# A fused attention and feed-forward kernel on one core: a new written-out order, with GpSimd squares in the first batch alone and seven products for the first row pair

## The chip, the cores and the metric

The kernel runs on one core of a Trainium2 chip. The core has TensorE (matmuls, PE in the profile), VectorE (DVE), ScalarE (ACT), GpSimd (POOL), and SyncE (SP), which here only issues transfers. Each engine takes its instructions strictly in the order of its own queue; a semaphore holds an instruction until what it needs is there. The metric is device time in microseconds of one execution; the median of three is given.

## The reference

Inputs q, k and v are 8 batches x 12 heads x 448 positions x 64. For each head, `scores = q k^T / 8`, `attn = max(scores, 0)^2 / 448`, `out = attn v`. The heads of a position are laid side by side to a row of 768, which gives 3584 rows. A feed-forward part follows: `h = x w_in` (768 to 2048), `g = h * sigmoid(1.702 h)`, `y = g w_out` (2048 to 768). Output is 3584 x 768 in float32. Products are in float16 with float32 sums.

## The kernel before

**Units.** Attention goes by units of four heads: 8 batches x 3 units, unit u = 3 * batch + part. A unit's 448 positions are seven blocks j of 64. For a unit, k and q are brought to float16 and transposed; then for each j four 64x64-tiled matmuls fill two PSUM banks with scores (`scores`, L143, word `s`), two ReLUs bring them to float16 in SBUF (`relu`, L156, word `r`, on ScalarE or VectorE), and one square in place makes the weights (`square`, L165, word `x`, on ScalarE, VectorE or GpSimd). When all seven are squared, `attn_v` (L173, word `a`) runs 28 matmuls, and `xt_evac` (word `e`) copies the result into the transposed activations of the feed-forward part.

**Ways in for k and q.** Units 0 to 5 load by a casting transfer on GpSimd's queue (`jk`, `jq`; unit 0 by SP and a cast) and transpose on TensorE (`tk`, `tq`) with a copy out (`ek`, `eq`). From unit 6 on SP loads float32 (`Lk`, `Lq`, one staging buffer each), an engine casts (`K`, `Q`; L107), and SP issues a DMA transpose (`Rk`, `Rq`). v is always a casting transfer on GpSimd's queue (`V`). Weights come by GpSimd's queue too (`jwa`, `jwb`, `jo`). The word `G` makes SP wait for a part of the weights, so that its later loads don't start earlier.

**Groups.** The feed-forward part takes positions in eight groups of 384 and 512 rows by turns (`gblk`, 6 and 8 blocks). The hidden layer of group 0, and half of group 1's, is a plain product (`m1`, word `f`); the rest uses seven products where eight would be needed: `unit_product` (word `u`, products 0 to 6) with sums of weights (`s_sum`, `S`) and of activations (`t_sum`, `T`) made beforehand, snapshots of a bank between products (`t`) and additions (`b`). Then gelu on ScalarE (`g`) and `widen`, a scaling into float16, on GpSimd (`v`).

**Output.** Rows go in tiles of 128. A pair of tiles takes seven products of eight matmuls (`pair_product`, L375, word `p`) with row sums on VectorE (`a_sum`, L357, word `A`), sums of the output weights (`w_sum`, `W`), copies out (`h`) and final adds (`l`). A tile without a partner is either plain (`m2`, word `m`, with `n` for the copy out: 16 matmuls for each half of the columns) or `single` (word `i`, also 16, with one sum `A.5` of its own). `o` and `q` issue the stores.

**Order.** There is no scheduler at run time: a string of some 1,900 words is the program. `do` (L441) executes them in turn, and each engine's queue is the subsequence of words that fall to it. A word is a name with numbers, then an engine after a colon where it isn't the default (a, d, p for ScalarE, VectorE, GpSimd), then PSUM banks after @. Defaults are in `home`: ScalarE for ReLUs, snapshots, copies out and k casts, GpSimd for widening and q casts, VectorE for the rest. There are eight banks; a word with @ waits until the bank's last reader is done. Tiles of a pool rotate over its buffers in the order in which the words ask for them.

Of the kernel before, what the change touches and what calls it, by code (L numbers as in the profile page):

```python
# [15 lines left out]
def kernel(  # L16
# [406 lines left out]
    with tc.manual_schedule():  # L423
# [35 lines left out]
        def zeros(e, p, n):  # L459
# [8 lines left out]
            "Lk0 z13@0 jk1 V1 jq1 I V0 K0:d tk0@1 z1 ek0 jk2 Lq0 Q0:a tq0@2 eq0 tk1@3 s0.3@4.5 "  # L468
            "r0.3.1 jq2 ek1 s0.1@6.7 r0.1.0 r0.3.0:d s0.0@0.1 s0.2@2.3 tq1@5 r0.0.1:d r0.2.0 "
            "s0.5@4.6 r0.1.1 s0.4@1.2 r0.0.0 r0.5.1 s0.6@7.0 eq1 r0.4.0:d tk2@5 x0.0 s1.0@1.6 "  # L470
            "r0.4.1 x0.4 jwb2 r0.5.0 x0.5 r0.6.1 jk3 r0.2.1 r0.6.0 x0.3:p jq3 x0.1 ek2 r1.0.1 "
            "r1.0.0 x0.2 x0.6 s1.5@2.4 s1.2@0.3 r1.2.0 s1.1@7.6 r1.1.1 tq2@5 a0@1.0 r1.1.0 r1.5.0 "
            "s1.6@6.7 eq2 r1.2.1 x1.0 r1.5.1 r1.6.0 s1.3@5.2 r1.3.0 x1.1 x1.2 tk3@3 e0.0.0 "
            "e0.0.1:a jk4 x1.5 e0.1.0:a tq3@4 r1.3.1 ek3 eq3 jwb0 x1.3 jq4 jwa0 s1.4@6.5 r1.6.1 "
            "V2 x1.6 r1.4.1 r1.4.0 s2.0@1.3 s2.2@2.7 r2.2.1 e0.1.1:a s2.1@4.5 r2.0.1 r2.0.0 "
            "r2.2.0 tk4@6 r2.1.1 x1.4 a1@7.0 e1.0.1:a ek4 r2.1.0:d x2.2 s2.6@3.6 r2.6.0 tq4@1 "
            "r2.6.1 e1.0.0 s2.3@2.4 r2.3.0 e1.1.1 x2.0 x2.1 eq4 s2.4@5.0 r2.3.1 jwa1 s2.5@3.6 "
            "f0.2.0@2 r2.4.0 r2.4.1 jwb1 jwa2 jq5 f0.3.0@4 s3.0@1.5 x2.6 e1.1.0 x2.3 f0.3.1 x2.4 "
            "jk5 r2.5.0 r2.5.1 x2.5 r3.0.0:d S0.1 V3 f0.2.1 f0.0.0@7 f0.0.1 s3.1@0.3 r3.0.1 "
            "a2@6.5 jwb3 r3.1.1:d r3.1.0 s3.2@1.0 e2.0.0 f0.1.0@3 e2.0.1:a r3.2.1 r3.2.0 G3 "  # L480
            "e2.1.1:a e2.1.0 x3.0 f0.1.1 f0.1.2 g0.1 x3.1:p V4 f0.2.2 s3.5@6.0 r3.5.0:d g0.2 "
            "s3.4@1.5 f0.0.2 v0.1 f0.3.2 r3.4.0 V5 r3.4.1 f0.4.0@3 r3.5.1:d x3.2 x3.5 g0.3 g0.0 "
            "f0.4.1 s3.3@2.6 s3.6@1.0 jwa3 f0.8.0@5 r3.3.1 r3.6.0 v0.0 r3.3.0 f0.4.2 g0.4 f0.8.1 "
            "f0.8.2 s4.1@4.7 s4.3@6.1 r3.6.1:d s4.0@0.2 f0.6.0@3 f0.6.1 r4.1.0 r4.3.1 x3.6 V9 "
            "f0.6.2 r4.3.0 x3.3 f0.5.0@4 r4.1.1:d r4.0.1:d x3.4 f0.5.1 S0.2 x4.1 f0.5.2 v0.4 "
            "s4.2@7.1 x4.3 a3@2.6 g0.8 g0.5 r4.2.1:d s4.4@5.4 r4.2.0 r4.0.0 tq5@7 g0.6 v0.2 jo1.0 "
            "Lk6 r4.4.0:d r4.4.1 tk5@0 eq5 s4.5@1.3 s4.6@4.5 ek5 e3.0.1:a f0.11.0@6 x4.2:a "
            "f0.7.0@7 f0.11.1 f0.11.2 r4.6.1:d r4.5.0 r4.5.1:d r4.6.0:d f0.10.0@0 f0.10.1 f0.7.1 "
            "x4.6 e3.0.0:a jo0.0 x4.5:a x4.4 f0.10.2 S2.1 g0.11 s5.1@1.5 s5.0@2.3 x4.0:p v0.5 "
            "f0.7.2 v0.11 f0.14.0@4 r5.0.1:d v0.6 f0.14.1 g0.10 r5.1.0 r5.1.1 r5.0.0 f0.14.2 "  # L490
            "jo0.1 S1.1 g0.14 g0.7 s5.4@6.0 a4@1.3 s5.3@5.2 r5.4.0:d v0.7 r5.3.0 e4.0.0:a "
            "s5.2@4.7 r5.4.1:d r5.2.1:d f0.12.0@6 x5.0:p e4.0.1:a f0.13.0@0 r5.2.0:d f0.12.1 "
            "f0.12.2 x5.4:a g0.12 v0.3 f0.15.0@5 f0.15.1 s5.5@7.1 r5.5.1 s5.6@4.3 r5.3.1:d x5.3 "
            "r5.5.0:d r5.6.0:d f0.13.1 r5.6.1 jo1.1 f1.7.0@2 f0.13.2 f1.1.0@6 x5.1:p v0.12 v0.10 "
            "v0.14 K6:p x5.5:a g0.13 f0.15.2 f1.5.0@1 f1.5.1 f1.7.1 S2.2 S2.4 x5.2:a x5.6:a "
            "f0.9.0@7 f0.9.1 f0.9.2 f1.4.0@3 S2.3 g0.15 g0.9 a5@4.0 e5.0.1:a f1.0.0@5 f1.0.1 "
            "f1.3.0@7 f1.1.1 Lq6 Q6:a e5.0.0 T1.1 T1.2 S1.2 v0.13 f1.7.2 g1.7 f1.3.1 v1.7 v0.9 "
            "Lq7 f1.3.2 f1.4.1 f1.4.2 f1.5.2 Rk6 u1.2.0@0 f1.6.0@4 Rq6 S3.1 g1.5 f1.6.1 g1.3 "
            "f1.2.0@2 f1.0.2 f1.6.2 v1.3 v0.15 t1.2.0 S3.3 g1.0 v0.8 g1.6 v1.0 Lk7 T1.4 S3.2 g1.4 "
            "u1.2.2 S3.4 W2.1 f1.2.1 f1.2.2 S1.4 u1.3.0@1 v1.4 W1.1 Q7:a f1.1.2 g1.1 v1.5 v1.1 "  # L500
            "u1.2.1@7 b1.2.1 g1.2.1 v1.2.1 v1.6 m0.0.0@5 u1.2.3 g1.2 s6.2@4.3 T1.3 Lq8 t1.3.0 "
            "s6.1@6.2 u1.3.2 S0.3 t1.2.2 n0.0.0:a r6.2.0 u1.2.4 r6.1.1:d r6.2.1:d s6.0@5.4 r6.0.1 "
            "r6.0.0 x6.0:a t1.3.2 V11 t1.2.4:d W0.1 u1.3.1@2 W2.2 Rq7 W0.2 m0.0.1@3 K7:p Q8:a "
            "b1.3.1 b1.2.3 g1.2.3 Rk7 u1.2.5 u1.2.6 u1.3.4 r6.1.0 W3.1 S0.4 v1.2 V7 u1.3.3 g1.2.5 "
            "v1.2.3 s6.4@4.5 s6.3@6.0 S1.3 n0.0.1 t1.3.4 g1.3.1 b1.2.6 b1.3.3 s6.5@3.7 r6.4.0 "
            "u1.3.5 x6.1:p r6.3.0:d r6.4.1:d r6.5.0 W1.2 v1.3.1 v1.2.5 u1.3.6 Lk8 g1.3.5 W3.2 V6 "
            "x6.4:a r6.3.1:d x6.2:a r6.5.1 Rq8 b1.3.6 K8:p m0.1.0@4 s6.6@6.3 W2.4 v1.3.5 g1.3.3 "
            "v1.3.3 s7.2@5.1 g1.2.6 x6.3 W1.4 v1.2.6 Lq9 g1.3.6 s7.0@0.2 r7.2.1 r7.0.0 x6.5:a Q9 "
            "r6.6.1:d r7.2.0:d Lk9 r7.0.1 m0.1.1@7 r6.6.0:d n0.1.0:a Rk8 s7.1@3.1 x6.6 W3.4 "
            "x7.0:a a6@5.0 s7.3@6.2 r7.1.0:d r7.1.1 n0.1.1 Lq10 s7.4@4.3 x7.2 e6.0.1:a K9:p "  # L510
            "r7.3.1 e6.1.1:a e6.0.0 r7.4.0:d p1.0.0@1 o0.0 r7.4.1:d e6.1.0:a s7.6@7.2 s7.5@0.5 "
            "r7.3.0 x7.1 x7.3 r7.6.0 r7.6.1:d r7.5.0 s8.2@4.6 m0.2.0@3 r7.5.1 r8.2.0:d V10 x7.4 "
            "s8.1@7.0 x7.6 r8.2.1 x7.5:a h1.0.0 n0.2.0:a s8.0@5.6 r8.1.1 a7@2.4 v1.3.6 r8.0.1 "
            "A1.0.1@0 A1.0.2@1 s8.3@3.0 W0.4 r8.3.0 r8.1.0:d e7.0.1 e7.1.1:a r8.3.1 p1.0.1@6 "
            "s8.5@7.3 V8 e7.0.0:a r8.0.0:d x8.1 e7.1.0 r8.5.0:d Rk9 r8.5.1 Rq9 s8.6@4.5 x8.0 x8.2 "
            "r8.6.1 x8.3:a p1.0.2 x8.5 r8.6.0:d s8.4@0.2 r8.4.1 s9.0@3.7 r8.4.0 l1.0.1 r9.0.0 "
            "x8.6 r9.0.1 x8.4 x9.0:a m0.2.1@5 n0.2.1:a s9.1@2.4 A1.0.4 r9.1.1:d Lk10 r9.1.0 "
            "a8@0.3 s9.2@7.5 e8.0.0:a Q10:d e8.0.1:a s9.3@4.2 r9.2.1:d r9.3.1 K10:p p1.0.3 "
            "u2.0.0@5 r9.2.0 Rk10 u2.1.0@2 Lk11 K11:p T2.1 W3.3 e8.1.0 T2.2 T2.3 e8.1.1:a "
            "s9.4@7.3 u2.0.1@0 W1.3 r9.4.1:d t2.0.0 u2.0.2 b2.0.1 t2.1.0 u2.1.2 u2.1.1@3 r9.3.0:d "  # L520
            "b2.1.1 W0.3 T2.4 r9.4.0 t2.0.2 u2.0.3 u2.0.4 g2.0.1 v2.0.1 t2.1.2 u2.2.0@7 g2.1.1 "
            "t2.0.4 b2.0.3 Lq11 t2.2.0 v2.1.1 u2.1.4 t2.1.4 h1.0.2 x9.2 u2.1.3 b2.1.3 u2.2.1@4 "
            "u2.0.6 g2.0.3 v2.0.3 b2.2.1 x9.4:a u2.2.2 u2.1.6 b2.0.6 g2.2.1 g2.0.6 Rq10 W2.3 "
            "u2.2.3 u2.3.0@0 Q11:a b2.1.6 t2.2.2:d u2.0.5 v2.0.6 g2.1.6 u2.3.1@3 g2.1.3 t2.3.0:d "
            "b2.3.1 v2.1.6 v2.2.1 u2.2.4 u2.1.5 u2.3.2 u2.3.3 t2.2.4 u2.2.5 A1.0.3 b2.2.3 u2.2.6 "
            "Lk12 o0.1 g2.3.1 t2.3.2 v2.3.1 v2.1.3 g2.0.5 g2.1.5 v2.0.5 u2.3.4 p1.0.4 g2.2.3 "
            "g2.2.5 s9.6@5.2 v2.1.5 b2.2.6 s9.5@4.7 t2.3.4:d u2.3.5 x9.1:a v2.2.3 K12 Lq12 b2.3.3 "
# [147 lines left out]
```

## Time and profile before

| | |
|---|---|
| median of 3 runs | 369.43 us (369.36 to 370.56) |
| the profiled execution's own time | 369.32 us |
| its span, first to last instruction | 367.5 us |
| granted TensorE clock | 0.998 |
| TensorE busy, 3570 matmuls | 357.2 us |
| VectorE busy | 290.2 us |
| ScalarE busy | 276.8 us |
| GpSimd busy | 179.0 us |
| HBM read and written | 45.6 and 11.0 MB |

A busy time is the union of the engine's instructions, so instructions that overlap count once. In a row of the timeline or of the groups, `at<-sc` means that tile `at` is written from tile `sc`: `sc` scores, `at` weights, `av` attention output, `xe`/`xo` activations of even and odd groups, `ht`/`hx` hidden layer in PSUM, `gf` the same in SBUF, `ge`/`go` after widening, `ox`/`op`/`os` outputs of pairs, plain tiles and singles, `osb` outputs in SBUF, `asum` row sums, `winS`/`wT` weight sums. All matmuls of the feed-forward part have the helper's line L203, all two-input sums L88.

### The profile page before, as it was taken

To read this page: it belongs to the slowest core of one execution; us is meant where nothing else is said; L and a number is where in the kernel's file an instruction comes from. 1 tells how busy PE (TensorE), PEld (TensorE's weight loads), DVE (VectorE), ACT (ScalarE), POOL (GpSimd) and SP (SyncE) were. 2 spreads that over 40 slices of the span, in tenths; PEclk is the share of its full clock that TensorE was granted. 3 is DMA by queue.
4 is the path that set the end of the run, shared out by engine and by line. 5 is a ranking of instruction groups with operands and counts; after the bars stand their busy time and mean duration, and the time that the engine had idled before them with its cause. 6 is when DMAs were issued, how large, how long until landed. Compare 5 with 4: busy or idle time off the path is not lost.

```text
span 367.5 us, 9086 instructions
## 1 busy us (share of the span) xinstructions
PE 357.2 (97%) x3570; PEld 231.1 (63%) x3570; DVE 290.2 (79%) x519; ACT 276.8 (75%) x542; POOL 179.0 (49%) x229
## 2 busy tenths in 40 slices
PE   7899999999999999999999999999999999999994
PEld 4454545664569555886559755786549755787662
DVE  3999968599997877878898788767887899755642
ACT  3998976687888998889958898878995897174310
POOL 6838695674115585256404856367342536043300
PEclk9999999999999999999999999999999999999999
DMA  9999999799964885978583396368943042300244
GB/s 197 195 205 204 241 209 219 129 172 207 130 179 118 165 236 98 204 164 186 102 167 73 98 199 136 102 146 162 239 98 77 0 112 28 87 0 2 70 114 119
DMA packets 65228, 51.39 MB, mean 140 GB/s; under 512 B 35745, under 2 KB 61857, under 8 KB 65185
## 3 DMA queue, kind: packets, MB, share of 16 engines
q1 hardware_dynamic: 48256, 36.32, 42.4%
q0 software_dynamic: 16608, 14.09, 25.5%
q8 instruction: 28, 0.46, 0.5%
q10 hardware_dynamic: 320, 0.39, 0.4%
q14 instruction: 16, 0.12, 0.1%
HBM read 45.61 MB, written 11.01 MB: 154 GB/s over the span
## 4 chain that ended last, share of the span: by engine, by line
PE 84%; DVE 10%; ACT 2%; DMA 1%; issue 1%; POOL 1%; SPq 0%; POOLq 0%; DVEq 0%; ACTq 0%
PE hx L203 29%; PE ox L203 26%; PE sc L150 9%; PE ht L228 7%; PE av L181 7%; PE os L203 4%; DVE at L88 3%; PE op L203 3%; DVE at L161 2%; ACT at L163 2%; DVE wT L88 1%; DMA qst<-in_q_dram 1%; DVE asum L88 1%; POOL ge L217 1%; POOL at L88 1%
## 5 line engine op out<-in xcount | busy, mean ns | idle before, releaser
L163 ACT ACTIVATE at<-sc 128x448 f16<-128x448 f32 x215 | 104.7, 567 | 13.2 <-PE sc L150 12.8
L161 DVE TENSOR_SCALAR at<-sc 128x448 f16<-128x448 f32 x121 | 71.8, 618 | 12.9 <-PE sc L150 12.5
L217 POOL TENSOR_SCALAR go<-gf 128x512 f16<-128x512 f32 x64 | 41.6, 650 | 64.0 <-ACT gf L214 47.2
L88 DVE TENSOR_TENSOR gf<-hx,gf 128x512 f32<-128x512 f32 (+1 forms) x78 | 47.9, 627 | 26.8 <-PE hx L203 14.2
L203 PEld LDWEIGHTS <-win 128*128 128x128 f16 x624 | 56.4, 98 | 8.4 <-issue 2.8
L88 POOL TENSOR_TENSOR at<-at 128x896 f16<-128x896 f16 x27 | 45.7, 1694 | 29.8 <-ACT at L163 18.0
L217 POOL TENSOR_SCALAR ge<-gf 128x384 f16<-128x384 f32 x64 | 35.8, 559 | 45.9 <-ACT gf L214 28.7
L169 ACT ACTIVATE at<-at 128x896 f16<-128x896 f16 x57 | 53.9, 955 | 0.9 <-DVE at L161 0.6
L150 PE MATMUL sc<-qT,kT 64*64 64x448 f16 x672 | 52.4, 359 | 2.2 <-DVE at L161 0.6
L88 DVE TENSOR_TENSOR at<-at 128x896 f16<-128x896 f16 x84 | 53.7, 673 | 0.8 <-ACT at L163 0.4
L214 ACT ACTIVATE gf<-gf 128x512 f32<-128x512 f32 (+1 forms) x78 | 43.2, 579 | 9.4 <-DVE gf L88 9.4
L203 PE MATMUL ox<-wout,go 128*128 128x384 f16 x256 | 46.5, 327 | 0.0
L203 PEld LDWEIGHTS <-winS 128*128 128x128 f16 x468 | 42.7, 98 | 4.5 <-issue 1.0
L203 PEld LDWEIGHTS <-go 128*128 128x128 f16 x320 | 29.9, 98 | 22.6 <-issue 4.8
L203 PEld LDWEIGHTS <-ge 128*128 128x128 f16 x288 | 27.5, 98 | 19.7 <-issue 3.3
L79 ACT ACTIVATE gf<-hx 128x512 f32<-128x512 f32 (+1 forms) x51 | 27.2, 543 | 15.3 <-PE hx L203 7.2
L203 PE MATMUL hx<-T,winS 128*128 128x256 f16 (+1 forms) x312 | 37.0, 261 | 0.0
L181 PE MATMUL av<-at,v 64*64 64x448 f16 x672 | 36.2, 350 | 0.6 <-DVE at L88 0.4
L150 PEld LDWEIGHTS <-kT 64*64 64x64 f16 x672 | 17.7, 105 | 27.9 <-issue 23.5
L203 PE MATMUL hx<-xo,win 128*128 128x256 f16 x252 | 32.1, 273 | 0.0
L203 PE MATMUL ox<-wT,asum 128*128 128x384 f16 x176 | 31.8, 327 | 0.0
L203 PEld LDWEIGHTS <-asum 128*128 128x128 f16 x200 | 18.7, 98 | 15.3 <-issue 3.1
(78 smaller groups left out, 481.6 us busy)
## 6 DMA issues: line engine op xcount, KB each, us to landing
out_dram<-osb SPq DMA_DIRECT2D x52, 192.0 KB, 3.3
kst<-in_k_dram SPq DMA_DIRECT2D x19, 448.0 KB, 5.2
qst<-in_q_dram SPq DMA_DIRECT2D x19, 448.0 KB, 4.2
v<-in_v_dram POOLq DMA_DIRECT2D x24, 224.0 KB, 5.4
win<-in_moe_w_in_dram POOLq DMA_DIRECT2D x8, 384.0 KB, 9.5
wout<-in_moe_w_out_dram POOLq DMA_DIRECT2D x4, 768.0 KB, 12.3
k<-in_k_dram POOLq DMA_DIRECT2D x5, 224.0 KB, 6.5
q<-in_q_dram POOLq DMA_DIRECT2D x5, 224.0 KB, 6.0
```

The source lines that it names most:

```text
L79: nc.scalar.activation(out=o, in_=i, func=AF.Copy)
L88: eng[e].tensor_tensor(out=o, in0=x, in1=y, op=op)
L150: nc.tensor.matmul(out=sc[a][c, 0:S], lhsT=st["kT"][r, j, c], rhs=st["qT"][r, :, c], start=True, stop=True)
L161: nc.vector.tensor_scalar(out=o, in0=i, scalar1=0.0, scalar2=None, op0=ALU.max)
L163: nc.scalar.activation(out=o, in_=i, func=AF.Relu)
L169: nc.scalar.activation(out=at, in_=at, func=AF.Square)
L181: nc.tensor.matmul(out=av[s][64 * a:64 * a + 64, 0:S], lhsT=v16[r, a, 64 * j:64 * j + 64], rhs=at[r, a, :], start=(j == 0), stop=(j == J - 1))
L203: nc.tensor.matmul(out=o, lhsT=lhs(i), rhs=rhs(i), start=start and i == 0, stop=i == n - 1, skip_group_check=True)
L214: nc.scalar.activation(out=o, in_=i, func=AF.Gelu_apprx_sigmoid, scale=1.0 / SC)
L217: eng[e].tensor_scalar(out=o, in0=i, scalar1=SC, scalar2=1.0, op0=ALU.mult, op1=ALU.mult)
L228: nc.tensor.matmul(out=hp[g, f][:, 0:n], lhsT=w[:, i, fo:fo + 128], rhs=xts[g][:, i, 0:n], start=i == 0, stop=i == NK - 1)
```

## The change

Only the string of words changes (1,939 words before, 1,950 after). Functions stay as they are. Three things differ in the words.

Squares on GpSimd (`x...:p`) stay in the first batch alone, units 0 to 2: four, where 27 lay over the whole program. Casts of k and q (`K`, `Q`) may go to any of three engines. Group 0's three output tiles, plain before (`m0.*`, `n0.*`), become one pair in seven products and one single:

```diff
-            "x6.4:a r6.3.1:d x6.2:a r6.5.1 Rq8 b1.3.6 K8:p m0.1.0@4 s6.6@6.3 W2.4 v1.3.5 g1.3.3 "
...
+            "l0.0.1 u1.3.3 u1.2.6 s6.3@1.7 W0.4 x6.1:a p0.0.2 W1.3 b1.2.6 Rq8 g1.2.3 r6.3.0:d "
+            "t1.3.2 s6.5@4.1 A0.0.4 h0.0.2:d r6.3.1 u1.3.4 W0.3 v1.2.3 p0.0.3 Q7:a v1.6 r6.5.0 "
...
+            "v1.3.1 b1.3.3 x6.3 V7 s6.4@1.6 r6.4.0 p0.0.4 u1.3.6 h0.0.4:d u1.3.5 Rq7 r6.6.1 "
+            "l0.0.3 r6.4.1:d b1.3.6 p0.0.5 g1.2.6 g1.3.5 s7.4@7.1 s7.0@4.6 g1.3.6 g1.3.3 v1.3.3 "
```

And all words stand in a new order, with new banks and, in part, other engines. The first words:

```diff
-            "Lk0 z13@0 jk1 V1 jq1 I V0 K0:d tk0@1 z1 ek0 jk2 Lq0 Q0:a tq0@2 eq0 tk1@3 s0.3@4.5 "
-            "r0.3.1 jq2 ek1 s0.1@6.7 r0.1.0 r0.3.0:d s0.0@0.1 s0.2@2.3 tq1@5 r0.0.1:d r0.2.0 "
...
+            "jq1 z13@0 Lk0 I K0:d tk0@1 ek0 z1 Lq0 Q0:a tq0@2 tq1@3 jk1 eq0 s0.1@4.5 jwb2 jk2 "
+            "s0.6@6.7 s0.4@0.1 r0.4.0:d r0.6.0 tk1@2 ek1 jq2 jq3 eq1 s0.3@6.0 r0.1.1 r0.4.1 "
```

Counted over the whole program:

| words | before: ScalarE / VectorE / GpSimd | after |
|---|---|---|
| squares `x` | 57 / 84 / 27 | 72 / 92 / 4 |
| ReLUs `r` | 215 / 121 / 0 | 201 / 135 / 0 |
| casts `K`, `Q` | 14 / 2 / 22 | 16 / 4 / 18 |
| snapshots `t` | 51 / 27 / 0 | 44 / 34 / 0 |
| row sums `A` | 0 / 47 / 0 | 0 / 52 / 0 |
| copies out `h`, `n`, `l.5` | 35 / 21 / 0 | 37 / 19 / 0 |
| adds at the end `l` | 0 / 33 / 0 | 0 / 36 / 0 |
| matmuls of group 0's output | 96 of 384 columns | 88 of 384 columns |

In the first batch, up to the word `a2` ScalarE had 39 ReLUs and no square, VectorE 5 ReLUs and 20 squares, GpSimd 1 square; after, ScalarE has 31 ReLUs and 5 squares, VectorE 15 and 12, GpSimd 4 squares.

## The prediction

> **What bounds the kernel now.** I read the page first: the busy shares and the 40 slices.
>
> ```profile
> PE 357.2 (97%) x3570; PEld 231.1 (63%) x3570; DVE 290.2 (79%) x519; ACT 276.8 (75%) x542; POOL 179.0 (49%) x229
> ...
> PE   7899999999999999999999999999999999999994
> ...
> DVE  3999968599997877878898788767887899755642
> ACT  3998976687888998889958898878995897174310
> ```
>
> TensorE is busy 97%, but [...] this share hides stalls. The chain of waits gives issue rates instead: 8 matmuls of 384 columns take 1.30 us (0.163 each), 4 score matmuls 0.19, the 28 of one attention product 1.32, a 192-column matmul 0.083, a 256-column one 0.109. Times the counts in the groups, all matmuls need about 336 us (168 score groups 31.9, 24 attention products 31.7, transposes and warm-up 8.5, 504 + 588 gated products 106, first group's hidden layer 26, 808 output matmuls 131). The span is 367.5; the tail after the last matmul is 4.8 us and the head 1.2. So some 25 us are stalls. Stretches cut at the attention products of units 2, 3, 5, 6 and 8 (PE, PEld, DVE, ACT, POOL busy) show where:
>
> ```profile
> 0.00:26.70 26.70, 22.69 (x318) 12.39 (x322) 21.03 (x41) 20.57 (x46) 17.41 (x28) 1.00 1.13 199
> 26.70:36.70 10.00, 9.81 (x104) 4.79 (x100) 9.89 (x18) 8.24 (x20) 7.55 (x11) 1.00 1.26 204
> 53.60:86.30 32.70, 32.31 (x253) 19.50 (x253) 25.16 (x41) 23.99 (x43) 20.91 (x27) 1.00 0.97 174
> 86.30:103.20 16.90, 16.21 (x164) 8.45 (x167) 16.83 (x32) 12.96 (x29) 4.25 (x5) 1.00 1.05 162
> ```
>
> First place: from the first cast at 4.3 us to 36.7 us VectorE has no idle time to speak of, while the matmuls there need some 25 us. VectorE sets the start. Second place: 77 to 103 us, VectorE full again (16.83 of 16.90). From 103 to 313 us TensorE sets the pace with 1 to 2 us of stall per stretch; the last 50 us are TensorE alone.
>
> The groups give the prices of what the change moves between engines (busy, then mean ns of one):
>
> ```profile
> L163 ACT ACTIVATE at<-sc 128x448 f16<-128x448 f32 x215 | 104.7, 567 | 13.2 <-PE sc L150 12.8
> L161 DVE TENSOR_SCALAR at<-sc 128x448 f16<-128x448 f32 x121 | 71.8, 618 | 12.9 <-PE sc L150 12.5
> L88 POOL TENSOR_TENSOR at<-at 128x896 f16<-128x896 f16 x27 | 45.7, 1694 | 29.8 <-ACT at L163 18.0
> L169 ACT ACTIVATE at<-at 128x896 f16<-128x896 f16 x57 | 53.9, 955 | 0.9 <-DVE at L161 0.6
> L88 DVE TENSOR_TENSOR at<-at 128x896 f16<-128x896 f16 x84 | 53.7, 673 | 0.8 <-ACT at L163 0.4
> ```
>
> These overlap by about 0.1 us when they follow each other. In the timeline 19 ReLUs of ScalarE take 8.40 us, so one costs (8.40 - 0.57)/18 = 0.435; two ScalarE squares take 1.81, so 0.855 for the second; three VectorE squares 1.69, so 0.535; two VectorE ReLUs 1.16, so 0.54. Moving a square from VectorE to ScalarE frees 0.535 and costs 0.855; the ReLU that goes back frees 0.435 and costs 0.54.
>
> VectorE squares average 673 ns, 55 above their usual 618. The timeline shows why:
>
> ```profile
> 10.62 2.86 DVE L88 TENSOR_TENSOR at<-at 128x896 f16<-128x896 f16 x4
> ...
> 29.00 1.80 DVE L88 TENSOR_TENSOR at<-at 128x896 f16<-128x896 f16 x1
> ...
> 78.83 2.60 DVE L88 TENSOR_TENSOR wT<-wout,wT 128x768 f16<-128x768 f16 x2
> ```
>
> Four squares should take 3 x 0.535 + 0.618 = 2.22, and take 2.86 while a GpSimd square runs (9.68 to 11.39). One alone takes 1.80 beside a GpSimd square from 28.65. Two weight sums, which should take 1.02, take 2.60 beside GpSimd widenings. Summed over all VectorE operations that read two SBUF tiles, the lengthening is 11.8 us: 3.2 beside GpSimd squares, 4.7 beside widenings, 1.5 beside casts, the rest not clearly placed.
>
> [...]
>
> **The change, part by part.**
>
> Group 0's first pair. Before, three plain tiles: 3 x 2 x 16 = 96 matmuls of 384 columns. After: 7 x 8 = 56 for the pair, 2 x 16 = 32 for the tile left over, 88. Saved 8 x 0.163 = 1.3 us, where TensorE sets the pace. Added on VectorE: five sums of 0.60 (3.0 us, between 55 and 90 us), and three fused adds for copies (near nothing). The pair also needs the sums of the output weights (16 x 0.47 = 7.5 us) some 20 us earlier. Those weights are four loads of 12.3 us from issue to landing; the last is now asked for behind more widenings, so the first sums may wait 1 to 2 us on VectorE. Nothing waits behind them then: in the 10 us that follow VectorE has 4 us less work than TensorE. I count 0 (to +1).
>
> The first batch. Counted in order of issue up to unit 2's attention product: VectorE has 1 cast, 10 transposed copies, 5 ReLUs and 20 squares (36 x 0.535), a weight sum and four small copies: 20.9 us. After: 1, 10, 15 and 12 (38 x 0.535) and three copies: 21.4. ScalarE goes from 39 ReLUs to 31 ReLUs and 5 squares: 18.8 to 19.7. GpSimd squares there go from 1 to 4. Each of the two seen by 30 us lengthened VectorE, by 0.64 and 1.18; three more at 0.6 each, since not every one meets a square, add 1.8. So VectorE reaches that point 0.5 + 1.8 = 2.3 us later. Bounds: nothing, if the three meet ReLUs [...]; 4, if each costs 1.2. By unit 5's product TensorE has been the bound in the old kernel with 3 us of VectorE slack, so a part is given back: I take **+1.5** (0 to +3). Loads don't decide: the new GpSimd queue asks for q and k of units 1 to 3 before v, and at the old 1.1 us per load v of unit 0 lands near 15 us, ahead of its use.
>
> 53 to 103 us. GpSimd loses the square at 76.15 that stood among blocked weight sums. Against that, five sums, and every square after batch 0 on the other two. Counting issue costs between the products of units 5 and 8: VectorE 37.3 before, 39.6 after, TensorE's bare columns 44.1 and 43.7. Before, VectorE's work came late and was lengthened by 4.8 us, most of it between 77 and 90 us; after, it is spread evenly. I take **-0.5** (-2.5 to +2).
>
> Steady stretches. GpSimd drops 23 squares (37 us); 15 go to ScalarE, 8 to VectorE, and 14 ReLUs and 7 snapshots pass from ScalarE to VectorE. VectorE's issue total rises 264 to 284 us, ScalarE's 256 to 262: both below TensorE's 326 bare columns, so the cover holds on average. It is thinnest between the products of units 12 and 14: VectorE 17.0 us, ScalarE 15.6, bare TensorE 15.3, in 16.9 us before (there VectorE 13.5). Early work in the stretch before must hide it. **+0.7** (-0.5 to +2.5).
>
> Banks. A bank is free about 0.2 us after its last matmul's columns plus the copy (0.49 to 0.69) plus 0.05: 0.75 to 0.96. Counting TensorE work between the last write of a bank and its next use beyond 60 us, the old order has nothing under 0.96. The new has nine places at 0.56 to 0.85 (after unit-product 2.2.4, single product 4.2.1, pair products 5.0.5 and 5.0.6 and others). Deficits of 0.1 to 0.3 each: **+0.8** (+0.2 to +2).
>
> SP's queue. Casts k and q change engines, and unit 7's q comes late: its cast stands after the product 0.0.3 on ScalarE, then SP must issue unit 9's q load (0.4) and the DMA transpose (4.1 us to landing): 0.95 + 0.4 + 4.1 = 5.5 us. TensorE has 4.2 us of columns before unit 7's first scores; everything behind them on TensorE waits. The cast can run up to 1.3 us early. **+0.3** (0 to +1.5). Other units have over 6 us.
>
> Tail: same last products, one evacuation and stores. 0.
>
> Sum: -1.3 + 1.5 - 0.5 + 0.7 + 0.8 + 0.3 = +1.5 us. The profiled run took 369.3 us (span 367.5 and 1.8 around it), 0.1 under the median of 369.43, so the change stands for both: 369.4 + 1.5 = **370.9 us**.
>
> **Rivals.** (1) Faster, by one mechanism: VectorE's blocked time. If the early GpSimd squares cost VectorE nothing (unit 2's product starts by 27 us) and the spread of weight sums takes out the 77 to 103 us plug (-2.5), and the last three entries come to 1.0 instead of 1.8, the sum is -1.3 + 0 - 2.5 + 1.0 = -2.8: 366.6. It decides from 0.8 us saved in the plug on: -1.3 - 0.8 + 1.0 = -1.1. For it: 4.8 of the 11.8 us of lengthening lie around that plug. Against: five more sums on the same engine. (2) VectorE and ScalarE become the bound in the attention stretches: with 17.0 of VectorE work where 16.9 us passed, six stretches lose 0.7 more each: 375. Against: the average slack. (3) Nothing measurable: the start's loss is given back before unit 5, as TensorE then has work stored up: -1.3 + 0.3 - 0.5 + 0.7 + 0.8 + 0.3 = +0.3, 369.7.
>
> **Numbers.** My forecast (slower by 0.3 to 1%) 0.43, rival 2 0.14, rival 3 0.25, rival 1 0.18. A measurement of this kernel can tell 0.3% (1.1 us) from no change. Faster 0.18, same 0.25, slower 0.57. The range reaches to half of rival 1 and all but the worst of rival 2: 367.8 to 374.5; the forecast's own range is 370.5 to 373.
>
> **What will show it.** In the new profile: 88 matmuls into the group-0 output, unit 2's attention product near 29 us (26.7 before) with VectorE squares over 1 us beside GpSimd squares; GpSimd near 140 us busy; VectorE busy over 295; a TensorE wait before unit 7's first scores near 83 us; short waits after the nine bank places. Wrong, if unit 2's product comes by 27 us, or if the last stretch (313 us on) moved by itself.

## The result, and the profile after

The changed kernel takes 370.71 us (median of 20 runs, 367.98 to 374.67); the old one, run beside it, 369.77 us (20 runs, 368.98 to 372.12). The ratio of comparable runs is 0.9999, 95% interval 0.9978 to 1.0021: no difference that can be measured. Four of the changed kernel's runs, 374.0 to 374.7 us, were in a slow state and don't count in the ratio; the first profile was taken in one of them (374.0 us, granted clock 0.987), so unless said otherwise "the changed kernel" is read from a second execution of the same words (370.7 us, span 368.9, clock 0.993; 22 more runs, median 370.61, ratio 1.0004, interval 0.9982 to 1.0025).

Its page, lines of parts 1, 2 and 5:

```profile
PE 357.8 (97%) x3562; PEld 232.7 (63%) x3562; DVE 302.2 (82%) x556; ACT 281.2 (76%) x540; POOL 136.9 (37%) x202
...
PE   8699999999999999999999999999999999999994
...
DVE  3978996999987889787997989798897899856452
ACT  3979985789988999889897898778887899245210
...
PEclk9989999999999999999999999999999999999999
...
L88 DVE TENSOR_TENSOR at<-at 128x896 f16<-128x896 f16 x92 | 56.7, 638 | 1.7 <-ACT at L163 0.6
```

Work moved as counted: 8 matmuls fewer, GpSimd from 179 to 137 us, VectorE from 290 to 302. VectorE's squares average 638 ns where they took 673. But in the third slice, 18 to 28 us, VectorE and ScalarE fall from 9 and 9 to 7 and 7: they wait where they were full. And there the granted clock is below 0.9 (0.50 from 19.0 to 22.4 us).

The same execution cut at the attention products of units 2, 3, 5, 6 and 8 (the columns are again PE, PEld, DVE, ACT, POOL busy, then clock, DMA share and GB/s):

```profile
0.00:30.76 30.76, 24.92 (x318) 13.01 (x318) 21.96 (x43) 22.14 (x44) 20.78 (x29) 0.94 1.13 193
...
57.78:88.98 31.20, 31.12 (x247) 18.42 (x250) 28.27 (x50) 23.88 (x45) 14.71 (x22) 1.00 0.89 179
88.98:104.20 15.22, 15.22 (x165) 7.94 (x160) 13.79 (x28) 14.74 (x29) 5.59 (x8) 1.00 0.95 217
```

Unit 2's product stands at 30.76 us instead of 26.70, with as many matmuls before it (318). The stretch from unit 5 to unit 8 takes 46.42 us (31.20 + 15.22) where it took 49.66 (53.57 to 103.23), and VectorE is no longer full in its second part (13.79 of 15.22). So "no change" is a loss and a gain of the same size. Starts of TensorE's groups, from the traces:

| start of, us | before | changed | difference | changed, first profile |
|---|---|---|---|---|
| unit 2's product | 26.68 | 30.76 | +4.1 | 30.30 |
| unit 5's product | 53.57 | 57.78 | +4.2 | 57.33 |
| unit 8's product | 103.23 | 104.20 | +1.0 | 107.56 |
| last matmul | 362.54 | 363.94 | +1.4 | 367.11 |

The first profile loses almost 4 us more between units 5 and 8, most of it at one place, to which the last experiment comes back.

What TensorE waited for between 8 and 35 us, in the list of waits (us in total, times, longest):

```profile
PE tr L131 <- DMA q<-in_q_dram: 1.3, 1, 1.3
PE av L181 <- DMA v<-in_v_dram: 0.9, 1, 0.9
PE tr L131 <- DMA k<-in_k_dram: 0.9, 1, 0.9
```

Three loads lead the list; the two entries below them are 0.6 and 0.2 us. In the same window of the old kernel only one load stood there, with 0.3 us:

```profile
PE sc L150 <- DVE kT L83: 0.4, 1, 0.4
PE tr L131 <- DMA q<-in_q_dram: 0.3, 1, 0.3
```

By the trace TensorE was ready for q of unit 2 at 12.9 us, for k of unit 3 at 15.7 and for v of unit 0 at 17.5; they landed at 14.2, 16.6 and 18.4. In the old order q of unit 2 landed at 12.5, k of unit 3 at 16.2 but was wanted only after unit 0's product, and v of unit 0 was there at 9.8. An input-weight block, asked for third on GpSimd's queue, now stands ahead of them.

And the contention that the prediction put on the first batch is not there. GpSimd's squares, then VectorE, in the timelines of the changed kernel:

```profile
17.97 1.71 POOL L88 TENSOR_TENSOR at<-at 128x896 f16<-128x896 f16 x1
...
25.12 5.41 POOL L88 TENSOR_TENSOR at<-at 128x896 f16<-128x896 f16 x3 [3.07 <-ACT at L163]
```

```profile
23.50 2.22 DVE L88 TENSOR_TENSOR at<-at 128x896 f16<-128x896 f16 x4
...
26.17 2.77 DVE L161 TENSOR_SCALAR at<-sc 128x448 f16<-128x448 f32 x5
```

Four squares take 2.22 us, the undisturbed time that the prediction worked out. From 25.12 to 30.53, while GpSimd squares, VectorE finishes the last of the four and then has ReLUs and copies from PSUM, which keep their usual lengths: five ReLUs in 2.77 us (4 x 0.54 + 0.62 = 2.78), two more in 1.16, copies of 0.61 and 0.62. Beside the single square from 17.97 it has one copy of 0.61 us.

### The profile page after: what moved, and what is told of

It is laid out like the page before. It is cut to its first block, busy times and chain, and to the rows that moved or that the text cites. A ratio compares the mean times of both kernels' runs of the same rounds, so it can differ in the third digit from the quotient of the medians.

```text
span 372.2 us, 9025 instructions
## 1 busy us (share of the span) xinstructions
PE 358.6 (96%) x3562; PEld 233.2 (63%) x3562; DVE 302.9 (81%) x556; ACT 281.3 (76%) x540; POOL 137.6 (37%) x202
## 4 chain that ended last, share of the span: by engine, by line
PE 84%; DMA 7%; DVE 3%; POOL 2%; ACT 1%; issue 1%; SPq 0%; DVEq 0%; ACTq 0%
PE ox L203 30%; PE hx L203 27%; PE sc L150 9%; PE av L181 8%; PE os L203 6%; DMA wout<-in_moe_w_out_dram 4%; PE ht L228 3%; DMA v<-in_v_dram 2%; DMA qst<-in_q_dram 1%; DVE wT L88 1%; PE tr L131 1%; POOL ge L217 1%; DVE at L88 1%; ACT gf L214 1%; POOL go L217 0%
## 5 line engine op out<-in xcount | busy, mean ns | idle before, releaser
L163 ACT ACTIVATE at<-sc 128x448 f16<-128x448 f32 x201 | 99.6, 559 | 13.0 <-PE sc L150 12.7
L161 DVE TENSOR_SCALAR at<-sc 128x448 f16<-128x448 f32 x135 | 79.8, 618 | 10.9 <-PE sc L150 10.6
L169 ACT ACTIVATE at<-at 128x896 f16<-128x896 f16 x72 | 68.2, 962 | 1.7 <-DVE at L161 1.2
L88 DVE TENSOR_TENSOR at<-at 128x896 f16<-128x896 f16 x92 | 55.9, 631 | 1.7 <-ACT at L163 0.6
L181 PE MATMUL av<-at,v 64*64 64x448 f16 x672 | 37.5, 357 | 1.0 <-DMA v<-in_v_dram 1.0
L203 PEld LDWEIGHTS <-ge 128*128 128x128 f16 x256 | 24.0, 98 | 18.4 <-issue 4.1
L79 ACT ACTIVATE gf<-hx 128x384 f32<-128x384 f32 (+1 forms) x44 | 23.3, 537 | 15.4 <-PE hx L203 12.0
L203 PE MATMUL ox<-wT,asum 128*128 128x384 f16 x192 | 34.9, 327 | 0.0
L203 PEld LDWEIGHTS <-asum 128*128 128x128 f16 x224 | 21.1, 98 | 16.3 <-issue 3.3
L81 ACT ACTIVATE osb<-ox 128x384 f32<-128x384 f32 x32 | 15.4, 496 | 19.2 <-PE ox L203 19.1
```

The source lines that it names most:

```text
L79: nc.scalar.activation(out=o, in_=i, func=AF.Copy)
L81: nc.scalar.activation(out=o, in_=i, func=AF.Copy, scale=scale)
L88: eng[e].tensor_tensor(out=o, in0=x, in1=y, op=op)
L161: nc.vector.tensor_scalar(out=o, in0=i, scalar1=0.0, scalar2=None, op0=ALU.max)
L163: nc.scalar.activation(out=o, in_=i, func=AF.Relu)
L169: nc.scalar.activation(out=at, in_=at, func=AF.Square)
```

## The experiments

Theory: the order of the first 30 us, with its loads, costs some 3 to 4 us, and the rest of the changed kernel is better than the old one by as much. Rivals: the elementwise engines set the start (the prediction's step); the losses were accidents of one execution; the squares' engines decide. All diffs are of words; a word that moves is shown at both places. Ratios are to the old kernel, with 95% intervals.

### The changed kernel again

No edit.

> The changed kernel once more, nothing edited, for a profile at full granted clock (the first one had 0.987) and a second interval. Theory A (the losses seen in the first profile, 3.2 us before 30 us and 2.7 us at 68 us, belong to the order of words): both are there again, TensorE reaches the attention product of unit 8 some 3 to 4 us later than before's 103.2, and the time is within 0.5% of before only because something later is better by as much. Theory B (they belong to that one disturbed execution): unit 8's product comes within 1 us of 103.2 us and the output weights land before 62 us. Ratio to before 0.998 to 1.004 either way.

Measured: ratio 1.0004 (0.9982 to 1.0025), the tables above. Unit 8's product came at 104.20. So the 4 us at 68 us of the first profile belong to that execution, and the loss at the start does not: the words for the first 30 us are the same in five of the traces here, and unit 2's product came at 29.24, 29.27, 30.30, 30.35 and 30.76, always 2.6 to 4.1 us behind the old kernel's 26.68. The granted clock has a part in this spread. The trace with 29.24 (the next experiment's) keeps 1.00 through the start; each of the other four has one stretch of 3.4 us at 0.50 there, which costs at most 1.7 us.

### Output weights earlier

```diff
-"... jo0.0 eq5 ... g0.11 jo0.1 v0.11 ... f1.1.0@7 jo1.1 f0.14.1 ... S3.1 jo1.0 f0.9.2 ..."
+"... jo0.0 jo1.0 jo0.1 jo1.1 eq5 ... g0.11 v0.11 ... f1.1.0@7 f0.14.1 ... S3.1 f0.9.2 ..."
```

> Only the four loads of the output weights are moved: the last three are asked for directly behind the first on GpSimd's queue, in the order in which the sums need them. Theory 1 (the last of them, landing at 66.2 us, holds the weight sums, and behind them on VectorE the snapshot that TensorE waits 2.7 us for): they land by about 55 us, the 2.7 us wait at 68 us is gone, and the kernel is 2 to 2.7 us faster than the changed one (ratio to before about 0.993). Theory 2 (VectorE is late there by its own work, not by the loads, or the stall moves to the next wait): 0 to 0.7 us faster. Theory 3 (the early weights take bandwidth from k, q and v of units 3 to 6): slower by up to 2 us.

Measured: 369.77 us, ratio 1.0000 (0.9969 to 1.0032). The last block landed at 60.5 instead of 64.6 us; units 5 to 8 took 46.65 instead of 46.42. Theory 2 holds where the load lands at 64.6, as in the second execution of the changed kernel: it is just in time.

### One block of input weights later

```diff
-"... Q0:a tq0@2 tq1@3 jk1 eq0 s0.1@4.5 jwb2 jk2 ... V2 a0@0.6 V1 x1.5:a ..."
+"... Q0:a tq0@2 tq1@3 jk1 eq0 s0.1@4.5 jk2 ... V2 a0@0.6 V1 jwb2 x1.5:a ..."
```

> Only one load is moved: the input-weight block that stands third in GpSimd's queue goes behind the v loads of units 0 to 2, so that q, k and v of the first units are asked for about 1.9 to 3 us earlier. Theory 1 (the order of loads sets the changed start: q of unit 2 at 13.2 us and v of unit 0 at 17.65 us were waited for): unit 2's attention product comes 1.5 to 3 us earlier and the kernel gains 1 to 2.5 us. Theory 2 (VectorE, ScalarE and three GpSimd squares in a row set it): unit 2's product moves by less than 0.7 us, the kernel by less than 0.7 us.

Measured: ratio 1.0043 (1.0022 to 1.0065), unit 2's product at 30.72. The wait for v went; those for q and k stayed at 1.1 and 0.9 us: q of unit 2 is asked for only at 7.7 us, when its buffer is free, and landed at 14.06 even without the weight block ahead. The move put the block ahead of another that the first hidden layer needs, and TensorE waited 0.7 us for that. A badly chosen place, and a miss for theory 1 as tested here.

### v of units 0 and 1 at once

```diff
-"... tq1@3 jk1 eq0 s0.1@4.5 jwb2 jk2 ... x0.3 V0 r1.5.1 ... V2 a0@0.6 V1 x1.5:a ... jwb1 e0.1.1:a"
+"... tq1@3 jk1 V0 V1 eq0 s0.1@4.5 jk2 ... x0.3 r1.5.1 ... V2 a0@0.6 x1.5:a ... jwb1 jwb2 e0.1.1:a"
```

> Only three loads move in GpSimd's queue: v of units 0 and 1 go directly behind k of unit 1, into the time in which the queue waits for a k buffer, and the input-weight block that stood there goes behind the other early blocks (its first use is near 36 us). Theory 1 (the order of the early loads is what makes the changed start late): q of unit 2 lands about 12.5 us instead of 14.2, v of unit 0 before 10, k of unit 3 about 14.7 instead of 16.6; the waits of 2.0, 1.1 and 1.1 us between 12 and 18 us go, unit 2's attention product comes at 28 to 28.8 us instead of 30.8, and the kernel is 1.5 to 2.5 us faster than the changed one (ratio to before 0.994 to 0.996). Theory 2 (squares and ReLUs on the slower engines set the start): unit 2's product stays above 30 us and the time within 0.7 us.

Measured: 373.18 us, ratio 1.0038 (1.0013 to 1.0063). In its trace (clock 1.0) the waits for q and v are gone and unit 2's product stands at 28.68, as theory 1 had it. Against the changed kernel's 30.76 that is 2.1 us, but 30.76 holds a stretch at half clock; against the 29.24 of the same start without one, the moved loads gain 0.6. What waits between 8 and 35 us now is

```profile
PE tr L131 <- DMA k<-in_k_dram: 1.1, 1, 1.1
PE sc L150 <- DVE at L161: 0.9, 2, 0.7
```

so k of unit 3 is late as before, and the stretch from unit 2's to unit 3's product grows from 9.73 to 11.08 us, 0.7 of it in a new wait for VectorE at 33.8 us. Unit 8's product comes at 103.68. The time did not follow the trace: 16 of its 22 executions had a mean granted clock under 0.997, with a median of 373.7 against 370.1 us for the other six. Why this order draws a lower clock more often is not settled. Two moved loads don't mend the start.

### Both moves together

The last edit and the early output weights in one kernel:

```diff
-"... jk1 eq0 s0.1@4.5 jwb2 jk2 ... V0 ... V1 ... jo0.0 eq5 ... jo0.1 ... jo1.1 ... jo1.0 ..."
+"... jk1 V0 V1 eq0 s0.1@4.5 jk2 ... jwb1 jwb2 ... jo0.0 jo1.0 jo0.1 jo1.1 eq5 ..."
```

> The moved early loads and the moved output-weight loads together. If the two are independent: as the previous kernel, and another 0 to 0.8 us less, 367 to 368 us (ratio to before 0.992 to 0.995). If the early output weights collide with the k, q and v that now come sooner, no faster than the kernel with the early loads alone.

Measured: 371.09 us, ratio 1.0017 (0.9994 to 1.0040). No gain; in its trace k of unit 3, landed at 17.7 us, held TensorE for 2.8 us, where the changed kernel has 0.9 with a landing at 16.6. Landing times at the start vary between executions of the same words: q of unit 2 came at 13.2 us in the changed kernel's first profile and at 14.2 in its second, v of unit 0 at 17.7 and 18.4. TensorE waited for v in both, 0.95 and 0.9 us.

### The pair of group 0 undone

```diff
-"A0.0.1@0 ... p0.0.0@3 h0.0.0 ... p0.0.1@2 ... A0.0.2@1 ... l0.0.1 ... p0.0.2 ... A0.0.4 h0.0.2:d ..."
-"p0.0.3 ... A0.0.3 ... p0.0.4 h0.0.4:d ... l0.0.3 ... p0.0.5 ... l0.0.5:a ... p0.0.6 ... l0.0.6"
+"A0.0.5@0 ... i0.0.0@3 n0.0.0:a ... i0.1.0@2 ... A0.1.5@1 ... n0.1.0:d ... i0.0.1@3 ..."
+"n0.0.1:d ... i0.1.1@2 ... n0.1.1:a"
```

> The pair of group 0 in seven products is undone inside the changed order: its two tiles become two more singles (64 matmuls of 384 columns where there were 56, two row sums where there were four, copies only in place of final adds). Theory 1 (TensorE sets the pace there, so each matmul counts 0.163 us): 1.3 us slower than the changed kernel. Theory 2 (VectorE, which loses two row sums of 0.6 us and three final adds, sets the pace there): 0 to 1 us faster. Theory 3 (both): within 0.5 us.

Measured: 374.34 us, ratio 1.0109 (1.0064 to 1.0155). Against the changed kernel's trace at the same clock (both 0.993), units 5 to 8 take 48.69 instead of 46.42 us, 2.27 more; the last matmul is 1.87 us later, as this execution reached unit 5 0.4 us earlier. Behind unit 8 both take 259.74 us. Eight more matmuls explain 1.3 of the 2.27; most of the rest is idle time of TensorE in the same stretch, 0.83 us between the products of units 5 and 6 where the changed kernel has 0.08. All six runs were at a clock of 0.994 or less, so the larger difference of the medians is not the products' alone. The seven products gain the forecast 1.3 us in matmuls, and here 0.75 us of idle time besides.

### Squares back on GpSimd

The edit has 26 words, 13 from VectorE and 13 from ScalarE; among them:

```diff
-"... x3.1 ... x4.0 ... x5.1:a ... x10.4:a ... x10.3:a ... x12.6 ... x23.0 ..."
+"... x3.1:p ... x4.0:p ... x5.1:p ... x10.4:p ... x10.3:p ... x12.6:p ... x23.0:p ..."
```

> In the changed order the 26 squares after unit 2 that the old kernel had on GpSimd go back there (12 from ScalarE, 14 from VectorE); order, banks and all else stay. Theory 1 (GpSimd squares cost VectorE time and are late, each 1.69 us against 0.62 or 0.96): slower by 0.5 to 2 us, with the attention stretches longer. Theory 2 (VectorE and ScalarE, with 20 and 6 us more work than before, were near the bound in the attention stretches): faster by 0.5 to 1.5 us. Theory 3 (TensorE covers both after 104 us): within 0.4 us, and unit 8 to the end takes 259.5 to 260 us as in the changed kernel.

Measured: 391.84 us, ratio 1.0573 (1.0535 to 1.0610): 21 us slower, far beyond all three theories. Its largest stall, in the timelines of TensorE and of GpSimd:

```profile
147.44 2.83 PE L181 MATMUL av<-at,v 64*64 64x448 f16 x28 [5.49 <-DMA v<-in_v_dram]
```

```profile
139.26 3.32 POOL L88 TENSOR_TENSOR at<-at 128x896 f16<-128x896 f16 x2 [7.61 <-ACT at L163]
...
143.49 0.78 POOL L104 DMA_DIRECT2D v<-in_v_dram  x1
```

GpSimd waited 7.61 us for the ReLUs of unit 10, made two squares, and only then reached the word `V10`, which asks for the v that unit 10's own product needs. The next largest sum in its list of TensorE's waits, 3.2 us, is for GpSimd's squares themselves, and four stretches of its trace, 17.1 us together, are at a granted clock of 0.50 (at most 8.5 us of the loss, some of which the changed kernel has too). The new order puts its loads into a queue in which no late square stands ahead of them. So the squares are not a separate part that can be put back: order and engines go together.

### Squares off GpSimd in the old order

The same 26 words, in the old string; among them:

```diff
-"... x3.1:p ... x4.0:p ... x5.0:p ... x10.4:p ... x10.3:p ... x12.6:p ... x23.0:p ..."
+"... x3.1 ... x4.0 ... x5.0:a ... x10.4:a ... x10.3:a ... x12.6 ... x23.0 ..."
```

> One part of the change alone: in the old order, the 26 squares after unit 2 that GpSimd has go to the engines that the changed kernel gives them to (14 to VectorE, 12 to ScalarE). Nothing else is changed. Theory 1 (GpSimd's squares lengthen VectorE's work and are late themselves, so that taking them away is a gain by itself): 1 to 2 us faster than before. Theory 2 (the gain or loss belongs to how the order was laid around the engines; in the old order VectorE and ScalarE get 7.5 and 10.3 us more where they were laid full): 1 to 4 us slower. Theory 3 (TensorE covers it): within 0.5 us.

Measured: 374.99 us, ratio 1.0143 (1.0122 to 1.0164), and all six executions at a clock of 0.997 or more. Taking the squares off GpSimd is a loss of 5 us by itself. Windows cut at the products of units 14, 15 and 23, first of this kernel, then of the old one:

```profile
189.03:215.03 26.00, 24.88 (x272) 18.99 (x265) 19.55 (x39) 21.68 (x44) 8.69 (x14) 1.00 0.49 106
215.03:318.53 103.50, 101.62 (x1036) 66.46 (x1035) 88.68 (x158) 86.45 (x167) 34.14 (x49) 1.00 0.50 112
```

```profile
188.18:212.53 24.35, 24.35 (x272) 18.99 (x268) 18.94 (x37) 19.83 (x41) 13.00 (x17) 1.00 0.49 106
212.53:313.00 100.47, 100.35 (x1040) 65.73 (x1032) 83.01 (x151) 83.82 (x164) 51.21 (x61) 1.00 0.52 117
```

Both stretches grow (by 1.65 and 3.03 us, and the one from unit 8 to 14 by 1.07, 86.02 against 84.95) and TensorE gets idle time that it did not have, though no engine is full over a stretch. Between the products of units 8 and 23 its list of waits starts with 1.6 us for VectorE's final adds (`osb`) and 0.9 us for VectorE's ReLUs, where the old kernel's has one entry, 0.3 us; which wait ends last at each place was not followed. Nothing is lost before unit 8 (103.01 against 103.23). The changed kernel carries 183.5 us of VectorE work between units 8 and 23, 10.7 more than the old one's 172.8 (70.86 up to unit 14, then 18.94 and 83.01), in 210.21 us against 209.77. So with the squares off GpSimd the changed order is some 5 us better than the old one; how much of that is order and how much the moved ReLUs and snapshots was not separated.

### The old start, the changed rest

The old kernel's 153 words up to unit 2's product with banks renamed, then the changed order without what is done; the joint in between (words after `a2`):

```diff
+"e2.0.0 r3.1.0 S2.1 r3.1.1:d x3.0:a e2.0.1:a s3.2@4.5 r3.2.1:d f0.1.0@3 r3.2.0 f0.1.1 f0.1.2 e2.1.0:a"
+"g0.1 e2.1.1 s3.3@2.7 f0.0.2 r3.3.1:d V4 V5 jwb3 f0.2.2 r3.3.0 x3.2 jwa3 g0.0 g0.2 f0.3.2 g0.3 x3.3"
```

> The old kernel's first 153 words (all of its order, engines and loads up to unit 2's attention product; its banks are only renamed so that the open ones fit) in front of the changed order for all that follows. Theory 1 (the changed kernel loses about 3.5 us in its first 30 us through loads that come late for TensorE, and is better than the old one after that): unit 2's attention product is back near 26.7 us (30.8 in the changed order), unit 8's at 101 to 102 us (103.2 before, 104.2 changed), and the time 366 to 367.5 us: faster than both (ratio to before 0.989 to 0.994). Theory 2 (what the start loses is made up before unit 8 in any case, because TensorE has a store of ready work later): unit 8's product within 0.5 us of 104.2 and the time as the changed kernel's.

Measured: 373.27 us, ratio 1.0084 (1.0057 to 1.0111). A new stall of its own, in VectorE's and TensorE's timelines:

```profile
31.41 0.56 DVE L88 TENSOR_TENSOR winS<-win 128x768 f16<-128x768 f16 x1 [1.60 <-DMA win<-in_moe_w_in_dram]
```

```profile
32.56 0.38 PE L150 MATMUL sc<-qT,kT 64*64 64x448 f16 x3 [3.16 <-DVE at L161]
```

The weight sum `S2.1` waits for its load, and `r3.1.1`, which TensorE needs for a bank, stands behind it and starts at 31.88. It is not the only loss: the last output weights landed at 66.4 us, VectorE waited 3.1 us for them, and units 5 to 8 took 49.03 us where the changed kernel has 46.42. The test says nothing on the theories yet.

The same with the early output weights:

```diff
-"... jo0.0 eq5 ... jo0.1 ... jo1.1 ... jo1.0 ..."
+"... jo0.0 jo1.0 jo0.1 jo1.1 eq5 ..."
```

> The same with the last three loads of the output weights asked for directly behind the first. If they land in time in most executions anyway: equal to the kernel with the old start within 0.5 us. If with the earlier start the weight sums wait for them, as in the first profile of the changed kernel, 1 to 3 us faster than that kernel.

Measured: 372.52 us, ratio 1.0078 (1.0052 to 1.0103), within 0.8 us of the kernel before. The weights land at 61.7 us and units 5 to 8 take 46.16 us, so the second loss is gone. The stall at the joint is there again, 3.81 us, now with 6.8 us at a granted clock of 0.50 from 30.7 us on, which takes back most of it.

### The old start, joined better

```diff
-"e2.0.0 r3.1.0 S2.1 r3.1.1:d x3.0:a e2.0.1:a s3.2@4.5 r3.2.1:d f0.1.0@3 ..."
+"jwb3 r3.1.1:d r3.1.0 s3.2@4.5 e2.0.0 f0.1.0@3 e2.0.1:a r3.2.1:d r3.2.0 e2.1.0:a e2.1.1 x3.0:a"
+"f0.1.1 f0.1.2 s3.3@2.7 g0.1 f0.0.2 r3.3.1:d V4 V5 f0.2.2 r3.3.0 x3.2 jwa3 g0.0 g0.2 f0.3.2 g0.3 x3.3"
+"... r3.4.0 x3.4 x3.5 S2.1 x3.1 ..."
```

> The old start before the changed rest once more, joined better. In the first joining VectorE met a sum of input weights (S2.1) 1.6 us before its load had landed, with the ReLU behind it for which TensorE then waited 3.2 us; here that sum stands 15 words later and the ReLU ahead of it. Theory 1 (loads late in the changed start, the rest better): no TensorE wait over 1 us between 26 and 40 us, unit 2's product at 26.7 to 27.7, unit 8's at 101 to 102.5 us, and the time 367 to 368.5 us (ratio to before 0.992 to 0.997). Theory 2 (no gain to be had after the start, or the old start's late weights always push back): 369 to 371 us.

Measured: **367.94 us** (19 runs, 367.57 to 370.47), ratio **0.9951 (0.9935 to 0.9966)**: faster than both. Unit 2's product at 27.76, unit 5's at 55.63, unit 8's at 101.80, the last matmul at 361.46 us, 1.1 before the old kernel's and 2.5 before the changed one's. TensorE's waits between 8 and 35 us:

```profile
PE tr L131 <- DMA q<-in_q_dram: 1.3, 3, 0.9
PE ht L228 <- ACT at L163: 1.0, 1, 1.0
PE tr L131 <- DMA k<-in_k_dram: 0.6, 1, 0.6
```

"Faster than both" goes by the ratios to the old kernel, which ran beside each. With the changed start replaced, what the changed rest is worth appears in the time. The start as a whole, with its joint, is shown to cost the difference. That late loads are a large part of it is what the lists of waits say (3.1 us for loads in the changed kernel, 1.9 in this one, 0.3 in the old one), and the clock has a part: 18 of this kernel's 19 executions had a mean clock of 0.997 or more, 12 of the changed kernel's 22. No kernel with only the loads moved could show it.

### A load late on purpose

```diff
-"... S3.1 jo1.0 f0.9.2 g0.9 v0.9 ... g0.13 v0.13 a5@2.6 ..."
+"... S3.1 f0.9.2 g0.9 v0.9 ... g0.13 v0.13 jo1.0 a5@2.6 ..."
```

> The kernel with the old start, with one load made late on purpose: the fourth load of the output weights moves behind four more widenings in GpSimd's queue (issue near 56 us where it was 49.5). In the kernel without this edit it lands at 61.8 us and the snapshot behind the weight sums on VectorE ends 1.0 us before TensorE wants it. Theory 1 (a wait costs its own length): landing at 65 to 67 us, a TensorE wait of 2 to 4 us before the third product of unit-product group 1.3 near 68 us, and the time longer by the same 2 to 4 us. Theory 2 (a wait of TensorE of that length also lowers the granted clock afterwards): the time longer by 3.5 to 6 us, with a granted clock well under 1 in the 4 us behind the wait. Theory 3 (TensorE has other work to do or the loss is made up by unit 8): under 1 us.

Measured: 373.68 us, ratio 1.0133 (1.0116 to 1.0150), so 1.8% above the kernel without the edit. The load landed at 67.3 us. TensorE's timeline, then windows of four microseconds with the granted clock third from the end:

```profile
71.73 3.30 PE L203 MATMUL hx<-T,winS 128*128 128x256 f16 x18 [4.25 <-DVE gf L83]
```

```profile
68.00:72.00 4.00, 0.27 (x3) 0.24 (x3) 4.00 (x8) 0.90 (x3) 1.50 (x3) 1.00 1.05 238
72.00:76.00 4.00, 4.00 (x27) 2.26 (x26) 2.49 (x7) 1.24 (x3) 3.88 (x2) 0.57 1.08 215
```

A wait of 4.25 us, and then four microseconds at a mean clock of 0.57, which lose another 1.7 (4 x 0.43). Cut finer it is 0.50 for 3.4 us, from 72.5 to 75.9. The last matmul comes 5.2 us later than without the edit, after a start that was 0.4 earlier. Theory 2: this wait cost more than its length.

The first profile of the changed kernel has the same place without any edit, with the load landing at 66.2 us. VectorE, then TensorE:

```profile
66.32 1.03 DVE L88 TENSOR_TENSOR wT<-wout,wout 128x768 f16<-128x768 f16 x2 [3.85 <-DMA wout<-in_moe_w_out_dram]
...
68.29 0.96 DVE L88 TENSOR_TENSOR wT<-wout,wout 128x768 f16<-128x768 f16 x1
```

```profile
72.26 3.10 PE L203 MATMUL hx<-T,winS 128*128 128x256 f16 x15 [2.71 <-DVE gf L83]
```

VectorE is held 3.85 us, then its sums take 0.96 instead of 0.55 beside GpSimd's widenings, and the snapshot behind them comes 2.7 us late for TensorE, whose next 15 matmuls take 3.10 us; the clock is 0.50 from 72.6 to 76.0.

## Why the prediction was right and where it was wrong

The forecast time, 370.9, is 0.2 us from the median measured, and the range held it. But the old kernel measured 0.3 us higher beside it, and the likeliest case, slower by 0.3 to 1%, did not come: the outcome was "nothing measurable", to which it gave 0.25. And that came by another way than rival 3's, whose loss at the start was to be given back before unit 5. It was still 4.2 us there. That the time came within 0.2 us is luck in part: the start lost 2.6 us more than forecast, and the other terms were together better by about as much.

| step of the sum | forecast, us | measured, us |
|---|---|---|
| seven products | -1.3 | -2.3 (units 5 to 8 with and without, same clock) |
| first batch | +1.5 (0 to 3) | +2.6 to +4.1 in five traces |
| 53 to 103 us | -0.5 | -1.0 (46.42 - 49.66 = -3.2 in all, of which -2.3 go with the products) |
| steady stretches and banks | +0.7 and +0.8 | +0.4 together (259.74 against 259.31 from unit 8 to the last matmul) |
| unit 7's q on SP's queue | +0.3 | 0: TensorE is idle for 0.1 us before those scores |
| output weights | 0 (to +1) | 0 with the load at 64.6 us, 2.7 and 1.7 of clock with it at 66.2 |

**First batch: the step that failed.** "Loads don't decide: the new GpSimd queue asks for q and k of units 1 to 3 before v, and at the old 1.1 us per load v of unit 0 lands near 15 us, ahead of its use." In the five traces with this start it landed at 17.0 to 18.4, and in the changed kernel it was waited for, as were q of unit 2 and k of unit 3. The estimate left out that a load is asked for only when its buffer is free: q of unit 2 at 7.6 us whatever the order, with nothing but a weight block to fill the time before. The old order had v of two units there. Nor was TensorE's own order asked, which now wants k of unit 3 ahead of unit 0's product. The contention step (1.8 of the 2.3 us) measured nothing: its lower bound, "nothing, if the three meet ReLUs", was the case. Unit 2's product "near 29 us" came for the wrong reason: the squares of over 1 us, named as its sign, aren't there.

**Products: right in their matmuls;** the idle time that goes with them, 0.75 us, was not in the sum. **53 to 103 us: right in sign,** -1.0 for -0.5: the second stretch is no longer full for VectorE (13.79 of 15.22 us, 16.83 of 16.90 before). So the place that rival 1 named did get better, by less than the 2.5 us that it needed, and its first half, a start that costs nothing, failed.

**Steady stretches and banks.** The cover held, as forecast. From unit 8's product to the last matmul TensorE is idle for 0.43 us in all, 0.42 in the old kernel, and 0.41 of it is one wait for ScalarE at 167.9 us; so the short bank distances there cost at most that, and the 0.8 forecast for them is not there. A distance counted in bare columns is a lower bound of the time that passes, and the forecast took it as exact; that this is why the deficits did not appear is argued, not shown. Rival 2 (375 us) is refuted for the changed kernel; what the old order shows when the squares leave GpSimd, 375.0 us, has its size and looks like its mechanism, though it was not followed place by place. The prediction's reason against it, the average slack, is therefore no reason: the slack was there in both, and only one order used it.

**Output weights.** "Nothing waits behind them then" was wrong. A snapshot for TensorE stands behind the sums on VectorE, with about a microsecond to spare. Of the other traces with the changed order at that place only the first with the poor joint has such a wait (1.5 us); in the rest the load was in time.

**What the sum did not hold at all: the clock.** Waits were priced at their length, and here a stretch at half clock came on top. In the changed start TensorE is busy for 2.25 of the 4 us from 12 to 16 us and for 2.44 of the next 4, and the clock (third from the end) falls:

```profile
12.00:16.00 4.00, 2.25 (x40) 1.25 (x38) 3.89 (x8) 3.85 (x9) 1.71 (x4) 1.00 1.16 176
16.00:20.00 4.00, 2.44 (x42) 1.47 (x46) 2.58 (x5) 3.41 (x6) 4.00 (x5) 0.88 1.25 202
20.00:24.00 4.00, 3.94 (x52) 1.83 (x43) 3.17 (x7) 2.73 (x6) 1.70 (x3) 0.70 1.27 204
```

Cut finer, this is 0.50 for 3.4 us, from 19.0 to 22.4, a loss of at most 1.7 us. Over the 22 executions of the repeat, 10 had a mean clock under 0.997, with a median of 371.5 us; the other 12 had 369.3, where the old kernel's had 369.7 (45 of 51 were at 0.997 or more). So without the clock's part the changed kernel is level or slightly ahead; with it the profile at 0.993 shows +1.4.

## What to carry to other kernels

Before trusting a count of work per engine in a load-bound start, write down for every early load when its buffer is free, when it lands, and which instruction wants it first, in the new order of each engine. Moving work onto an engine that issues loads changes when those loads are asked for (`V10` stood behind a wait of 7.61 us and two squares); moving the squares' engine without the order cost 5 us in the old kernel and 21 us in the new one. And when a changed kernel measures the same, cut the trace at matching groups: here a start of +4 and a middle of -3 hid a version that is 0.5% faster than both.

## What the hardware showed beyond expectation

- **The price of a wait.** TensorE waits of 2.7 and 4.3 us were followed by 3.4 us at a granted clock of 0.50. One of 3.2 us was followed by no drop; beside one of 3.8 us stands a drop of 6.8 us, which began before the wait ended. So a wait's length alone doesn't tell. Windows of the two kernels with the poor joint, first the one with the 3.2 us wait, then the other:

```profile
28.00:32.00 4.00, 1.40 (x29) 0.61 (x21) 1.15 (x3) 1.78 (x3) 1.33 (x2) 1.00 1.25 205
32.00:36.00 4.00, 3.44 (x31) 1.49 (x31) 2.85 (x6) 2.60 (x8) 0.51 (x1) 1.00 1.28 208
```

```profile
28.00:32.00 4.00, 0.64 (x13) 0.14 (x5) 1.51 (x4) 1.21 (x2) 1.05 (x2) 0.83 1.25 204
32.00:36.00 4.00, 3.55 (x15) 1.29 (x16) 1.49 (x4) 1.51 (x4) 0.30 (x1) 0.50 1.26 204
36.00:40.00 4.00, 4.00 (x29) 1.81 (x27) 3.34 (x7) 3.31 (x8) 1.83 (x4) 0.81 0.93 155
```

  In the second kernel six matmuls of the hidden layer take 2.10 us at 0.50 (from 32.97 us) and 1.15 at 1.00 (from 41.00). No single long wait is needed: in the changed start the waits were of 0.9 to 1.3 us each.

  The first profile of the changed kernel tells more. Its three drops begin at 17.94, 72.56 and 369.51 us (the last one behind all matmuls), whole multiples of 3.41 us apart: 54.62 us is 16 x 3.41, and 296.95 is 87 x 3.41. Cut on that grid, the stretch of 3.41 us ahead of a drop had TensorE busy for 1.21, 0.70 and 1.33 us, that is 0.35, 0.21 and 0.39 of it. No other whole stretch of this trace had less than 0.72, and none was followed by a drop. The wait of 2.7 us (69.55 to 72.26) lay inside one stretch, the one with 0.21. Whether an edge of such a grid split the wait of 3.2 us was not shown. That the place of a wait on the grid is why its length doesn't tell is the author's guess from one trace; no experiment here moved a wait along it.
- **Scatter.** The changed start, whose waits change with the landings, gives 368.4 to 372.6 us in 22 runs; with the old start in its place 17 of 19 lie between 367.57 and 368.7. That fewer waits at the start, and fewer drops behind them, are why is argued from the clocks above.
